# An S4 convolution block with a bilinear GLU on one Trainium2 core: another hand-written order of the first stage's side jobs, with other ring buffers

## The chip, the core and the metric

The kernel runs on one core of one Trainium2 chip. The metric is the device time of the whole program in microseconds (us), from runs on the chip; a profiled execution of the same program is the source of every view shown. The engines are named as in the profile: PE (matmuls; PEld its weight loads), DVE (vector), ACT (activations), POOL (GpSimd), SP (which issues most DMAs).

## What is computed

One input of 2048 positions (S) with D = 640 channels goes through two residual branches, each with a layer norm and a modulation from a condition c; N = 192 states, F = 1536.

```python
mod = silu(c) @ w_mod                      # six rows sa, ca, ga, sb, cb, gb of 640
h = layernorm(x) * (1 + ca) + sa
dt = exp(log_dt); P = exp(dt * A * l)      # l = 0..2047, A complex (640 x 192)
K = real(einsum("dn,dnl,dn->dl", C, P, dt * B))
y = irfft(rfft(pad(h)) * rfft(pad(K)))[:2048] + h * Dskip
x = x + ga * y
h = layernorm(x) * (1 + cb) + sb
out = x + gb * (((h @ w_gate) * (h @ w_up)) @ w_down)
```

## The kernel before

The 640 channels are NB = 5 blocks of 128 (written db below). Stage 1 makes the convolution kernel K, the transforms and the first residual (x2d, kept in DRAM); it ends at about 551 us. Stage 2 is the gated unit in two halves of 1024 positions: the `pa` matmuls of L1057 and L1459. Its order is not touched.

**The main loop of stage 1** (`for t in range(3*NK+24)`) builds K in NK = 40 kernel groups of 16 channels, eight groups to a block, three steps `t` to a group `n`:

- POOL makes the tables of group n+1 (L708): `Ph` (phases, 1536 integers a partition, buffers Pha and Phb), `EQ` (1536) and `EP` (768), both with two buffers. `EQ` of group n+2 overwrites the one of group n, so it waits until QtB(n) has read it.
- ACT turns phases into sines and cosines (`tra`, `trb`, in PSUM; L229 is the helper that issues every activation). Steps 0, 1 and 2 of a group give those for `QtA`, `PtA` and for `PtB`/`QtB`.
- DVE multiplies: `QtA(n)` (L763 to L765), `PtA(n)` (L770), `PtB(n)` (L790), `QtB(n)` (L763 to L765 again).
- PE contracts them into `kg` (L805, L820); ACT copies the result to `Kta` or `Ktb`.

**Side jobs** run between the steps: a step t has two half-steps, 2t behind ACT's part and 2t+1 behind DVE's multiplies. A generator is made for each job, and the table `SCHED` gives the numbers at which it advances by one piece. Before the change such a number v belongs to half-step v // 10 and is also the order within it; negative ones belong to the prologue's steps, and half-steps from 243 on lie behind the last kernel group, where the number only sets the order. Nothing else plans: each engine executes its instructions in the order in which this program writes them, and an instruction whose input or buffer is missing holds up all that follow on its engine.

The jobs, by the keys of `SCHED`: `ml`, `mr` load w_mod and make the modulation rows (L354, PE L361, a copy on ACT to TVa or TVb); `st` loads a slice of x and takes its statistics (L463, DVE L471 and L472, two instructions and one); `hm` normalises and stores (L483); `rstd` turns statistics into factors (L277 to L284); `fo` is the fold: ten tiny transposing matmuls into a psf buffer (L380), a chain of 11 DVE operations on 128x5 (`mcol`, L384 to L394), matmuls of L401; `e0` the second half's exponentials (`LATE`, ACT: LP seven times, RH, RL); `q`, `mc`, `low` the seeds of a block (u_seeds, u_modc) and their tables (tab_ph, tab_eq); `pre` and `g` the forward transform of h; `k` (u_k, L842) that of K, whose result ACT copies to f16b; `c` (u_c: matmul L887, DVE L928 to L934, matmul L944, ACT copies to Wa or Wb, store to WD) product and inverse transform; `d` (u_d: loads TVa or TVb from WD L957 and x L959, matmul L965, addition L969 or L972, store to x2d L973) the last transform and the residual; `h`, `w` the gated unit's head (loads `xb` from x2d L1097, statistics L1105) and the first weights (L1000, `wga`). The last block's `c` is cut in two halves of 256 columns on DVE.

**Ring buffers** are chosen by hand too: `SLOT` has for each ring a string with one letter for each tile, in the order in which the tiles are made (psf, three PSUM buffers; TV, W, f16, gh, hf, Kt, Ph, PtA, ...). A job that moves takes another place in its strings.

Of the kernel before, what the change touches and what calls it, by code (L numbers as in the profile page):

```python
# [31 lines left out]
    ml=(-885, -911, -989),  # L32
    mr=(((-871, 89), (-871, 110)), ((-874, 26), (-884, 85)), ((-886, -866), (-888, -871))),
    st=(
        (-881, 51),
        (-1006, -914),
        (51, 229),
        (-884, 159),
        (-983, 0),
        (104, 215),  # L40
        (-936, -871),
        (-978, -871),
        (17, 200),
        (3, 193),
        (-911, -870),
        (-883, 63),
        (-871, 131),
        (-990, -906),
        (-883, 169),
        (-984, -870),  # L50
    ),
    hm=(
        (-1010, 359),
        (261, 368),
        (157, 359),
        (45, 328),
        (-988, 315),
        (32, 242),
        (303, 330),
        (-877, 240),  # L60
        (214, 259),
        (147, 306),
        (259, 375),
        (324, 407),
        (425, 536),
        (528, 544),
        (445, 539),
        (356, 434),
    ),
    rstd=(229, 229),  # L70
    tab=(526, 788),
    fo=(111, 124, 196, 224),
    e0=(150,),
    ds=(325, 213, 340, 438),
    mc=((-864, 219, 303, 339, 378), (-871, 395, 451, 466, 484), (349, 569, 607)),
    q=(
# [4 lines left out]
    ),  # L81
    pre=(
# [5 lines left out]
    ),  # L88
    c=(
# [5 lines left out]
    ),  # L95
    d=(
# [5 lines left out]
    ),  # L102
    k=(
        (167, 177),
        (309, 391),
        (675, 710),
        (452, 511),
        (433, 460),
        (480, 518),
        (603, 619),  # L110
        (619, 664),
        (674, 699),
        (829, 839),
        (902, 909),
        (1092, 1097),
        (956, 974),
        (969, 1054),
        (1067, 1070),
        (1080, 1080),
        (1260, 1292),  # L120
        (1259, 1267),
        (1453, 1476),
        (1414, 1426),
        (1473, 1485),
        (1417, 1434),
        (1505, 1574),
        (1489, 1495),
        (1606, 1624),
        (1687, 1714),
        (1877, 1897),  # L130
        (1882, 1908),
        (2012, 2039),
        (2018, 2077),
        (1960, 1963),
        (1984, 2016),
        (2097, 2137),
        (2350, 2377),
        (2212, 2252),
        (2289, 2315),
        (2481, 2546),  # L140
        (2430, 2519),
        (2474, 2543),
        (2515, 2552),
    ),
    low=((146, 404, 641, 884, 1117, 1399, 1630, 1871, 2090), (182, 429, 680, 921, 1134, 1399, 1634, 1859, 2096)),
    w=(2533, 2448, 2696, 2700, 2760, 2764),
    wm=(2850, 2860),
# [11 lines left out]
    Kt="abaaabaaababababbaabababa",  # L159
# [64 lines left out]
def tile_kernel(ctx: ExitStack, tc: tile.TileContext, I, out):  # L224
# [1418 lines left out]
```

## Time and profile before

| what | value |
|---|---|
| runs of the kernel | 1009.19, 1009.78, 1012.82 us, median 1009.78 |
| profiled execution: span; end of its last instruction | 1012.8 us; 1009.8 |
| busy of the span: PE, DVE, ACT, POOL | 897.8 (89%), 765.8 (76%), 574.4 (57%), 572.4 (57%) us |
| DMA | 153.16 MB, mean 151 GB/s |
| QtA(0) starts, QtB(39) ends on DVE | 30.73, 458.55 us |
| last store to WD, first addition of the last block's d | 502.88, 512.96 us |

How to read it: times in a timeline row are start and duration in us, then engine, line, operation, output <- input, shapes and count; the bracket behind says how long the engine sat idle before the instruction and what released it. The name of a tile leaves out its number, so EQ<-LQ,RH stands for both EQ buffers. The share of busy time is a mean over both stages. PE's busy time counts pipelined matmuls whose ends are modelled.

### The profile page before, as it was taken

Reading aid. Unit: us, or ns where it says so; the run is one execution under the profiler, and the core shown is the slowest. Engines: PE = TensorE matmul, PEld = TensorE weight load, DVE = VectorE, ACT = ScalarE, POOL = GpSimd, SP = SyncE. Lnnn points to the kernel's source line nnn. Section 1 sums busy time; section 2 is a strip of 40 time slices with the busy share of each in tenths; the row PEclk is TensorE's granted clock in tenths of the full one; section 3 lists DMA queues with packets and bytes.
Section 4 is the critical chain, followed back from the end, with each engine's and each line's share of the span. In section 5 each row is a group of like instructions: output and inputs, shape, how many; then the busy total and the mean of one; then the engine's idle time right before and its main releaser. Section 6 shows DMA issues by size and latency. Waiting matters only on the chain. (4 is left out here: it accounts for less than half of the span.)

```text
span 1012.8 us, 26818 instructions
## 1 busy us (share of the span) xinstructions
PE 897.8 (89%) x11192; PEld 732.0 (72%) x11192; DVE 765.8 (76%) x1389; ACT 574.4 (57%) x1049; POOL 572.4 (57%) x423
## 2 busy tenths in 40 slices
PE   4864798799789689988888999999999999999998
PEld 3653566576576467666746788889998888889998
DVE  8698578987989987893977977787576787768452
ACT  4759999987888897872437322234464422224331
POOL 4976899799869989950035576661112354452000
PEclk9876799999979989999999999999999999999999
DMA  7654665454445553558673444524644422221341
GB/s 243 236 140 151 235 230 151 161 163 130 142 129 159 168 150 104 179 170 283 209 208 94 151 134 136 191 109 130 211 157 160 152 79 82 86 67 54 103 157 52
DMA packets 147817, 153.16 MB, mean 151 GB/s; under 512 B 9200, under 2 KB 125424, under 8 KB 146288
## 3 DMA queue, kind: packets, MB, share of 16 engines
q1 hardware_dynamic: 145968, 148.43, 46.4%
q10 hardware_dynamic: 1728, 3.02, 0.8%
q8 instruction: 88, 1.44, 0.6%
q14 instruction: 33, 0.27, 0.1%
HBM read 110.45 MB, written 40.96 MB: 150 GB/s over the span
## 5 line engine op out<-in xcount | busy, mean ns | idle before, releaser
L708 POOL TENSOR_TENSOR EQ<-LQ,RH 128x1536 f32<-128x1536 f32 x40 | 124.2, 3106 | 23.0 <-DVE QtB L765 22.8
L229 ACT ACTIVATE z<-pa 128x512 f32<-128x512 f32 x24 | 14.4, 599 | 168.6 <-PE pa L1057 120.5
L1022 DVE TENSOR_TENSOR wsgl<-wga,wsgh 128x640 fp32r<-128x640 f32 x72 | 67.9, 947 | 45.7 <-ACT wsgh L229 45.6
L229 ACT ACTIVATE wsgh<-wga 128x640 fp32r<-128x640 f32 x72 | 52.6, 732 | 66.7 <-PE pa L1459 42.7
L1408 POOL TENSOR_TENSOR z<-z,s 128x512 f32<-128x512 f32 x24 | 33.6, 1400 | 92.9 <-DVE s L1407 92.9
L1034 POOL TENSOR_TENSOR tf<-wur,wgb 128x256 f32<-128x256 f32 x24 | 18.9, 785 | 93.1 <-DVE wtl L1022 57.7
L1459 PE MATMUL pa<-wsgh,sh 128*128 128x384 f32 (+1 forms) x304 | 69.7, 310 | 0.0
L1459 PE MATMUL pa<-wsgl,sh 128*128 128x384 f32 (+1 forms) x304 | 69.2, 309 | 0.0
L1459 PE MATMUL pa<-wsgh,sl 128*128 128x384 f32 (+1 forms) x304 | 69.1, 309 | 0.0
L708 POOL TENSOR_TENSOR EP<-LP,RH 128x768 f32<-128x768 f32 x40 | 66.1, 1652 | 0.0
L708 POOL TENSOR_TENSOR Pha<-LH,DH 128x1536 int32<-128x1536 int32 (+1 forms) x21 | 62.5, 2974 | 3.7 <-ACT trb L229 3.3
L708 POOL TENSOR_TENSOR Phb<-LH,DH 128x1536 int32<-128x1536 int32 x20 | 62.3, 3115 | 3.1 <-ACT tra L229 3.1
L1022 DVE TENSOR_TENSOR wtl<-tf,wth 128x256 fp32r<-128x256 f32 (+1 forms) x72 | 60.1, 861 | 0.0
L820 PE MATMUL kg<-QtB,PtB 64*32 64x64 f32 x2560 | 48.2, 227 | 4.9 <-DVE QtB L764 4.9
L820 PEld LDWEIGHTS kg<-QtB,PtB 64*32 64x32 f32 x2560 | 41.0, 113 | 12.8 <-DVE QtB L764 6.2
L1406 DVE TENSOR_TENSOR s<-pa,s 128x512 f32<-128x512 f32 x24 | 16.6, 690 | 44.6 <-PE pa L1057 39.6
L1057 PE MATMUL pa<-sh,wtl 128*128 128x512 f32 x144 | 45.1, 395 | 4.2 <-DVE wtl L1022 4.2
L1459 PEld LDWEIGHTS pa<-wsgh,sh 128*128 128x128 f32 x304 | 46.6, 188 | 0.0
L1459 PEld LDWEIGHTS pa<-wsgh,sl 128*128 128x128 f32 x304 | 46.6, 188 | 0.0
L1459 PEld LDWEIGHTS pa<-wsgl,sh 128*128 128x128 f32 x304 | 46.6, 188 | 0.0
L1057 PE MATMUL pa<-sh,wth 128*128 128x512 f32 x144 | 44.7, 391 | 0.0
L1057 PE MATMUL pa<-sl,wth 128*128 128x512 f32 x144 | 44.5, 390 | 0.0
(576 smaller groups left out, 2953.2 us busy)
## 6 DMA issues: line engine op xcount, KB each, us to landing
wga<-wdg SPq DMA_DIRECT2D x24, 640.0 KB, 5.2
wga<-B_w_gate SPq DMA_DIRECT2D x12, 640.0 KB, 4.8
wgb<-B_w_gate SPq DMA_DIRECT2D x24, 320.0 KB, 3.3
wur<-B_w_up SPq DMA_DIRECT2D x24, 320.0 KB, 4.0
xb<-x2d SPq DMA_DIRECT2D x6, 1280.0 KB, 7.2
TVb<-WD SPq DMA_DIRECT2D x26, 256.0 KB, 3.9
t_tw<-w_mod SPq DMA_DIRECT2D x3, 1600.0 KB, 8.0
t_ti<-w_mod SPq DMA_DIRECT2D x3, 1600.0 KB, 7.6
```

The source lines that it names most:

```text
L229: return S.activation(o, i, f, **kw)
L708: G.tensor_tensor(o.rearrange("p x (h l) -> p x h l", l=8), lo.unsqueeze(2).to_broadcast([P, rows, nh, 8]), hi.rearrange("p h x -> p x h") ...
L820: PE.matmul(kg[j * 32 : j * 32 + 32, dd, :], PtB[lo : lo + 64, c, r, :], QtB[lo : lo + 64, c, r, :], start=False, stop=dd == 7 and c == 1, ...
L1022: V.tensor_tensor(lo, v, hi, op=OP.subtract)
L1034: G.tensor_tensor(t[:, 0:2], u[:, 0:2], g[:, 0:2], op=OP.subtract)
L1057: PE.matmul(ps, w[a][:, k], x[b][:, l], start=n == 0 and m == 0, stop=n == 2 and m == len(ks) - 1)
L1406: V.tensor_tensor(S67[i], ps, S6[i], op=OP.add)
L1408: G.tensor_tensor(ZT[i], ZT[i], S67[i], op=OP.add)
L1459: PE.matmul(ACC[tb][t][c], x[:, ts], w[:, cs], start=st, stop=f == NF - 1 and n == 2 and (c == 0 or t % 2 == 1))
```

## The change

Only `SCHED` and `SLOT` are rewritten, and the half-step of a number is v // 1000 instead of v // 10, so that there are a thousand places within one. The five places in `SCHED` and the line that reads it which serve as an example:

```diff
-    ml=(-885, -911, -989),
+    ml=(4000, 5, -93000),
-    rstd=(229, 229),
+    rstd=(16000, 16002),
-    fo=(111, 124, 196, 224),
-    e0=(150,),
+    fo=(16007, 18007, 19004, 23000),
+    e0=(1,),
...
-            jobs.setdefault(v // 10, []).append((v, it))
+            jobs.setdefault(v // 1000, []).append((v, it))
```

All jobs move by some half-steps; the larger ones: two of the three w_mod loads and most modulation rows leave the prologue for half-steps 0 to 15, the x statistics are dealt out anew, `e0` goes from half-step 15 to 0, the four pieces of the fold from 11, 12, 19, 22 to 16, 18, 19, 23, the table loads t_tw and t_ti from 52 and 78 to 34 and 73, the last pieces of block 3's seeds (`q`) from 124 to 134 into 125 to 132, those of block 4 from 149 to 184 into 171 to 182, and of the last block's eight halves of `c` one more is done ahead of QtB(39). The counts of instructions stay (PE 2857 rows before and after, POOL 417, SP 331, ACT 962 and 961, DVE 1236 and 1238, where the two more are groups of like instructions that are no longer neighbours). The lines of the changed file are 28 higher (L763 is L791 there).

What stands on the engines now, at three places. First DVE in the prologue, behind the first multiplications of the seeds of block 0 (L554 to L557); gha is a slice of x, DL and DH are the words of the phase tables. Before:

```order
L557 TENSOR_TENSOR pta<-pta,psfb 128x192
L593 TENSOR_TENSOR ptb<-ptb,psfa 128x192
L573 CAST psfa<-psfc 128x192
L574 CAST DL_162<-psfc 128x4x24
L577 TENSOR_TENSOR DL_162<-psfa,shl 128x12x24
```

and now:

```order
L585 TENSOR_TENSOR pta<-pta,psfc 128x192
L499 BN_STATS st_235<-gha 128x6 x2
L500 BN_AGGR mv_95<-st_235 128x2
L621 TENSOR_TENSOR ptb<-ptb,psfb 128x192
L601 CAST psfb<-psfa 128x192
L602 CAST DL_162<-psfa 128x4x24
L605 TENSOR_TENSOR DL_162<-psfb,shl 128x12x24
```

The first slice's statistics, which stood behind the seeds of the first half, stand ahead of L593 (now L621) and of the phase words.

Second ACT in the steps of group 0 (ab, tra, trb belong to the sines; TVa, TVb are modulation rows). Before:

```order
L229 ACTIVATE trb<-Pha 128x512
L229 ACTIVATE trb<-ab,halfpi 128x512
L229 ACTIVATE ab<-Pha 128x512
L229 ACTIVATE tra<-Pha 128x512
L229 ACTIVATE tra<-ab,halfpi 128x512
L229 ACTIVATE TVb<-psfc 1x384
```

and now:

```order
L257 ACTIVATE trb<-Phb 128x512
L257 ACTIVATE trb<-ab,halfpi 128x512
L257 ACT_TABLE_LOAD
L257 ACTIVATE LP_148<-RL_158 128x96 x7
L257 ACTIVATE RH_155<-RH_155 128x1056
L257 ACTIVATE RL_158<-RL_158 128x288
L257 ACTIVATE TVb<-psfa 1x384
L257 ACTIVATE ab<-Phb 128x512
L257 ACT_TABLE_LOAD
L257 ACTIVATE tra<-Phb 128x512
L257 ACTIVATE tra<-ab,halfpi 128x512
```

The exponentials of the second half stand between the sines of QtA(0) and those of PtA(0), with a table load on either side; they stood two groups later.

Third PE behind the last kernel group (L965 and L993 are the d matmuls of the second to last block, L842 and L870 those of u_k, L887 and L915 those of c's halves on f16b). Before:

```order
L965 MATMUL psfa<-TVb,ct 32x512 x4
L842 MATMUL psfb<-ct,Ktb 64x128 x8
L842 MATMUL psfc<-ct,Kta 64x128 x8
L887 MATMUL psfa<-f16b,t_tw 64x64 x16
L842 MATMUL psfb<-ct,Ktb 64x128 x8
L965 MATMUL psfc<-TVa,ct 32x512 x4
L887 MATMUL psfb<-f16b,t_tw 64x64 x16
L887 MATMUL psfa<-f16b,t_tw 64x64 x16
```

and now:

```order
L915 MATMUL psfb<-f16b,t_tw 64x64 x16
L870 MATMUL psfc<-ct,Ktb 64x128 x8
L870 MATMUL psfa<-ct,Ktb 64x128 x8
L915 MATMUL psfc<-f16b,t_tw 64x64 x16
L993 MATMUL psfb<-TVa,ct 32x512 x4
L915 MATMUL psfa<-f16b,t_tw 64x64 x16
```

The d matmul that stood ahead of three u_k groups stands behind all of them, and behind four of the halves' matmuls in place of one; its input comes through TVa, as for the d matmul before it.

More of the change, by code (lines that the diff above doesn't have):

```diff
@@ L76 @@
-    q=(
[4 rows of a table removed]
+    ml=(4000, 5, -93000),
+    mr=(((8002, 10001), (8005, 15000)), ((5000, 8006), (6, 4001)), ((-87998, 3), (-87999, 9001))),
+    st=(
+        (8003, 10000),
+        (-100000, -91000),
+        (-87000, -86999),
+        (-87996, 7),
+        (-88000, -87997),
+        (10002, 13000),
+        (8, 2000),
+        (-97999, -95000),
+        (9, 6000),
+        (8004, 12000),
+        (-86998, 4),
+        (-87995, 2),
+        (-101000, -98000),
+        (9000, 15001),
+        (8000, 8001),
+        (-86997, 0),
+    ),
@@ new lines @@
+    hm=(
+        (16011, 16011),
+        (18009, 18009),
+        (18004, 18004),
+        (19000, 19000),
+        (16003, 16003),
+        (18005, 18005),
+        (11001, 16005),
+        (11000, 16004),
+        (28000, 35000),
+        (32000, 33000),
+        (16010, 18008),
+        (16012, 25002),
+        (47001, 51001),
+        (16013, 19003),
+        (26000, 32001),
+        (40003, 51002),
+    ),
+    rstd=(16000, 16002),
+    tab=(34000, 73000),
+    fo=(16007, 18007, 19004, 23000),
@@ L81 @@
+    e0=(1,),
+    ds=(40002, 35002, 25000, 48001),
+    mc=((10003, 18003, 18006, 19002, 19005), (16001, 25003, 27000, 38000, 44001), (51000, 55000, 60001)),
+    q=(
[4 rows of a table added]
     ),
     pre=(
[5 rows of a table removed]
-    ),
-    c=(
[5 rows of a table removed]
-    ),
-    d=(
[5 rows of a table removed]
-    ),
-    k=(
[L104 to L143, printed above, removed]
-    ),
@@ new lines @@
+    d=(
[5 rows of a table added]
+    ),
+    k=(
+        (18000, 18002),
+        (16008, 16009),
+        (49000, 50001),
+        (47000, 47002),
+        (48000, 48002),
+        (49001, 50000),
+        (54002, 54003),
+        (53000, 53001),
+        (64001, 66000),
+        (86000, 86001),
+        (79001, 79003),
+        (106002, 106004),
+        (94001, 94002),
+        (92000, 92001),
+        (100000, 102000),
+        (106005, 106006),
+        (127000, 127001),
+        (112002, 112003),
+        (139002, 140000),
+        (149000, 149002),
+        (139001, 139003),
+        (140003, 145001),
+        (149001, 149003),
+        (157001, 157003),
+        (166000, 170000),
+        (160000, 160001),
+        (182008, 184000),
+        (174000, 176000),
+        (205001, 206002),
+        (201002, 206001),
+        (196000, 196001),
+        (197000, 197001),
+        (208002, 208003),
+        (229001, 231001),
+        (221001, 223000),
+        (227003, 228000),
+        (287007, 287008),
+        (241000, 287001),
+        (287014, 287016),
+        (287015, 287018),
+    ),
@@ L155 @@
+    low=(
+        (16006, 43000, 64000, 91000, 115000, 139004, 163005, 184001, 206000),
+        (21001, 40001, 67003, 89000, 117002, 137003, 165001, 188000, 210001),
+    ),
+    w=(287005, 287067, 287038, 287042, 287044, 287048),
+    wm=(287041, 287057),
+    h=(287045, 287045, 287055, 287058, 287061, 287062, 287064, 287065),
+    g=(
[5 rows of a table added]
     ),
```

90 lines of the change are left out of this document (40 added, 50 removed), and 43 rows, old and new, of tables (c, d, g, pre).

## The prediction

> **What bounds the kernel now.** I read the page's sums first, then stage 1 stretch by stretch, then the waits at its two ends. The page: busy time per engine, POOL's line in 40 slices (25 us each), the chain that ended last.
>
> ```profile
> PE 897.8 (89%) x11192; PEld 732.0 (72%) x11192; DVE 765.8 (76%) x1389; ACT 574.4 (57%) x1049; POOL 572.4 (57%) x423
> ...
> POOL 4976899799869989950035576661112354452000
> ...
> PE pa L1057 25%; PE pa L1459 16%; DMA wga<-wdg 1%; PE psg L1132 0%; DMA wdg<-xb 0%; POOL xb L1503 0%; DVE wsgl L1022 0%; DVE wtl L1022 0%; DVE sl L1022 0%; POOL a L1426 0%; ACT wth L229 0%; DVE hl L1022 0%; ACT sh L229 0%; POOL tf L1036 0%; DVE xb L1474 0%
> ```
>
> The chain's 25% and 16% are stage 2, whose matmuls the change leaves in their order. So the question is when stage 2 starts (at about 551 us, where the last stretch below ends). The next table has the span's stretches in stage 1 (PE, PEld, DVE, ACT, POOL busy, granted clock, DMA share, GB/s).
>
> ```profile
> 290.00:365.00 75.00, 60.89 (x1548) 45.02 (x1546) 68.02 (x116) 63.36 (x116) 73.06 (x41) 0.93 0.52 154
> 372.00:442.00 70.00, 64.01 (x1554) 50.35 (x1553) 57.69 (x88) 55.81 (x96) 69.45 (x36) 0.95 0.50 152
> 458.00:551.00 93.00, 76.70 (x874) 54.31 (x867) 59.97 (x153) 40.58 (x74) 15.63 (x20) 0.98 0.63 193
> ```
>
> POOL is at 9 in the slices from 125 to 175 us, and it is the fullest engine of the next two stretches (73.06 of 75, 69.45 of 70): it builds the tables of one kernel group after another and only stops for its buffers. Behind 458 POOL is out of it, and DVE idles 33 of 93 us: there the order of the side jobs sets the end. So I sum three stretches: the start until POOL binds, POOL's part to the last group, and the tail from there to stage 2.
>
> **Start.** First DVE, SP and POOL in the prologue (start, duration, what), then the landing times of the gha loads.
>
> ```profile
> 8.96 0.35 DVE L557 TENSOR_TENSOR pta<-pta,psfb 128x192 f32<-128x192 f32 x1
> 9.76 0.35 DVE L593 TENSOR_TENSOR ptb<-ptb,psfa 128x192 f32<-128x192 f32 x1 [0.45 <-ACT psfa L229]
> 17.17 0.87 DVE L471 BATCH_NORM_STATS2 st<-f16a 128x6 f32<-128x320 f32 x2
> 18.08 0.21 DVE L472 BATCH_NORM_AGGREGATE mv<-st 128x2 f32<-128x12 f32 x1
> 30.73 1.18 DVE L763 TENSOR_TENSOR QtA<-trb,EQ 128x1024 f32<-128x1024 f32 x1
> ...
> 8.10 0.52 SPq L463 DMA_DIRECT2D f16a<-A_u  x1
> ...
> DMA to landing us min/median/max: 3.3/3.7/4.1
> ...
> 26.19 3.10 POOL L708 TENSOR_TENSOR EQ<-LQ,RH 128x1536 f32<-128x1536 f32 x1
> ```
>
> The first statistics of x now stand directly behind L557, ahead of L593. DVE is there at 9.3; the load is issued at 8.10 as before and lands 3.3 to 4.1 later, at about 11.8. That is 2.0 of wait (9.76 was the next start, after 0.45 of another wait) and 1.1 of work (17.17 to 18.29): **+3** for everything behind, L593, the DL and DH words and POOL's first tables. The same work is missing later in the prologue, but a second group now stands there, so nothing comes back before EQ of group 0: 29.2 instead of 26.19.
>
> The late exponentials now run in the first step on ACT. What they cost in the old place, and the fold in the old place on DVE with POOL beside it:
>
> ```profile
> 48.20 1.28 ACT L229 ACT_TABLE_LOAD   x1
> 49.49 1.45 ACT L229 ACTIVATE LP<-RL 128x96 f32<-128x96 f32 x7
> 50.73 1.09 ACT L229 ACTIVATE RH<-RH 128x1056 f32<-128x1056 f32 x1
> 51.73 0.42 ACT L229 ACTIVATE RL<-RL 128x288 f32<-128x288 f32 x1
> ...
> 50.16 0.17 DVE L384 TENSOR_SCALAR mcol<-psfb 128x5 f32<-128x5 f32 x1 [3.68 <-PE psfb L380]
> 52.83 3.01 DVE L388 TENSOR_TENSOR mcol<-mcol 128x5 f32<-128x5 f32 x1
> 57.64 1.21 DVE L763 TENSOR_TENSOR QtA<-trb,EQ 128x1024 f32<-128x1024 f32 x1
> ...
> 52.73 3.09 POOL L708 TENSOR_TENSOR EQ<-LQ,RH 128x1536 f32<-128x1536 f32 x1
> 67.86 3.10 POOL L708 TENSOR_TENSOR EQ<-LQ,RH 128x1536 f32<-128x1536 f32 x1 [4.00 <-DVE QtB L765]
> 82.70 3.10 POOL L708 TENSOR_TENSOR EQ<-LQ,RH 128x1536 f32<-128x1536 f32 x1 [7.06 <-DVE QtB L765]
> ```
>
> The block and a table load on either side take 1.28 + 1.24 + 1.0 + 0.42 + 1.28 = 5.2 us of ACT (start to start), now between the sines of QtA(0) and those of PtA(0), where DVE has little else. With 2 of the 3 above (QtA(0) itself waits for sines, not for EQ) PtA(0) is some 7 late and QtA(1), which waited 1.25 more, some 4: 45. How the rest of the catching up goes needs the price of a group's multiplies and of the normalising factors:
>
> ```profile
> 40.72 1.22 DVE L763 TENSOR_TENSOR QtA<-tra,EQ 128x1024 f32<-128x1024 f32 x1 [1.25 <-PE kg L805]
> 46.06 0.41 DVE L765 SCALAR_TENSOR_TENSOR QtB<-tra,EQ 128x256 f32<-128x256 f32 x1
> ...
> L279 DVE RECIPROCAL rs<-ry 128x6 f32<-128x6 f32 x1 | 0.2, 192 | 0.8 <-ACT ry L229 0.8
> ```
>
> A group's multiplies take 40.72 to 46.47, 5.7. After QtA(1) at 45 come 5.7 and three statistics groups of 1.1, so QtA(2) starts at about 54 instead of 57.64: the fold's wait for psfb (3.68) and its chain (50.16 to 57.64, 7.5) have left its front. Then 5.7, two statistics groups (2.2) and the factors (14 operations of about 0.2 and 1.1 of waits, 3): QtB(2) ends at 65, so EQ(4) starts there and not at 67.86. The fold now stands behind QtB(2): 7.5, to 72.5; then QtA(3) and its group (5.7) with the four first operations of the seeds (1.5) to 80, and 1.4 that I add for waits on PE, where the last mod row now stands between. EQ(5), released by QtB(3), starts at about 81.4 and not 82.70: **−1.3**. The bounds: +8.2 if nothing of 3 + 5.2 is made up, −6.8 if the fold costs 2 (11 operations of 0.17) and not 7.5. I take −1.3: the slow row (3.01) is the one that recurs, as follows.
>
> Why the fold's operations are slow is in the rows: L388 on 128x5 takes 3.01, from 52.83 to 55.84, and POOL's EQ runs from 52.73 to 55.82. In the new place it stands directly behind QtB(2), which is what releases EQ(4): the same coincidence, so I keep 7.5. The Trainium skill, "SBUF — State Buffer", section "SBUF: two separate sides", says that VectorE operations with two SBUF inputs and GpSimd operations lock one shared port pair for a whole instruction. The row agrees with it; by the rule alone, were POOL idle there, the sum would be some 5 us lower.
>
> **POOL's part.** What is late when POOL gets full, in the slices at 125, stays late while it is. Half-steps 40 to 120 hold nearly the same work per group before and after, so −1.3 is carried. The seeds of blocks 3 and 4 move by a few half-steps: block 3's tail now stands as one lump ahead of QtA(22), and the rows behind it are relieved by the same work. No row prices that; the nearest are POOL's 7.06 of idle at a lump of the same kind (before 82.70) from above and the same 7.06 given back from below. I halve it, ±3.5, and take 0, since the work is the same. At the end one half of the inverse transform of the last block and one addition are moved ahead of QtB(39). Their prices, and where the group loop ends:
>
> ```profile
> 458.13 0.42 DVE L765 SCALAR_TENSOR_TENSOR QtB<-tra,EQ 128x256 f32<-128x256 f32 x1
> ...
> 479.84 0.69 DVE L969 TENSOR_TENSOR xb<-psfa,xsb 128x512 f32<-128x512 f32 x1 [8.28 <-PE psfa L965]
> 480.45 0.41 DVE L928 TENSOR_TENSOR TVb<-psfc,f16a 128x256 f32<-128x256 f32 x1
> 482.57 0.41 DVE L934 TENSOR_TENSOR f16a<-TVb,psfc 128x256 f32<-128x256 f32 x1
> 499.14 0.41 DVE L934 TENSOR_TENSOR f16a<-TVb,psfc 128x256 f32<-128x256 f32 x1
> ```
>
> A half is 480.45 to 482.98, 2.5; an addition 0.6: **+3.1**. The last QtB ends near 458.55 − 1.3 + 3.1 = 460.4; I go on with 461.
>
> **Tail.** DVE's 8.28 ahead of 479.84 are its largest wait there. Who holds it up, and what follows (the landing times are those of the TVb loads):
>
> ```profile
> 477.14 2.66 PE L965 MATMUL psfa<-TVb,ct 64*32 64x512 f32 x8 [4.44 <-DMA TVb<-WD]
> ...
> 481.49 0.60 ACT L229 ACTIVATE f16b<-psfb 128x512 f32<-128x512 f32 x1 [7.83 <-PE psfb L842]
> 502.88 0.33 ACTq L949 DMA_DIRECT2D WD<-Wa  x1
> ...
> 466.17 0.91 SPq L1097 DMA_DIRECT2D xb<-x2d  x2
> 467.18 2.53 SPq L957 DMA_DIRECT2D TVb<-WD  x2
> ...
> DMA to landing us min/median/max: 9.7/9.8/9.8
> ...
> 507.71 0.91 SPq L957 DMA_DIRECT2D TVb<-WD  x2
> ...
> 512.96 0.69 DVE L969 TENSOR_TENSOR xb<-psfc,xsa 128x512 f32<-128x512 f32 x1 [3.25 <-DMA xsa<-A_u]
> ```
>
> PE runs in written order. Its d matmul on TVb waits until 477.14 for a load issued at 467.18 behind two xb loads; the three u_k matmul groups (L842) behind it feed ACT's f16b (7.83 idle), and those the halves. So one half is done before DVE's wait and seven after it, 480.45 to 499.55. After the change the waiting matmul stands behind all u_k groups: four halves can be done before it, three after. The waits: QtB(39) 461, four halves and an addition to 472; the load, issued when the d matmul ahead of it has read TVa (about 465.5), again behind xb, lands some 9.8 later, so DVE's xb addition is at about 478; two halves to 484, then a wait for the third d (its load behind the two wga loads) to about 488, the last half to 490.5, and the last WD store 3.3 later, as 499.55 to 502.88: 494 to 496 with a little for the psf buffers. That is −7 to −9 on 502.88. The last block's first load follows 4.8 later as now, and the addition 5.25 after it: 504 to 506 against 512.96. The statistics of the other rows lie beside that wait, as now. I take **−7** (the three of the half are in it, since it starts from 461). Bounds: −13 if the loads land in 4 us, 0 or a loss if they become the chain.
>
> The Trainium skill, "DMA: Bandwidth & Descriptors", section "Issuing engines are not separate DMA queues", says that transfers of all issuing engines interleave on the same 16 engines. By it the W stores, now moved earlier on ACT's queue, get no lane of their own beside the wga loads; the sum by it would be −3 and not −7 (the second rival).
>
> **The sum.** The tail's figure starts from 461, so the start's −1.3 and the half's +3.1 are in it already. Stage 2 starts 7 earlier and its order is kept, so 1009.8 − 7 = **1003**. The profiled execution spans 1012.8 and its last instruction ends at 1009.8, the same as the median shown (1009.78), so no shift is needed.
>
> **Rivals.**
> 1. *POOL's start is carried* (slower, 0.23). For: POOL is full soon after its EQ(5) (82.70), so what is late there stays. Price: the 3 + 5.2 that nothing makes up, +8.2 at EQ(5) in place of −1.3, and the half's +3.1: the last QtB ends at 470. From there to stage 2 it is 551 − 458.5 = 92.5 today and 544 − 461 = 83 by my tail, so stage 2 starts at 553, +2; if the fold also keeps its wait of 3.7, +6: 1015. It decides from EQ(5) later than about 89. Against: 7.06 of idle before EQ(5) today.
> 2. *The loads are the chain* (no change, 0.21). Three d loads in a row now use the same buffer TVa, so each waits for the d matmul before it and lands up to 9.8 later; the last block's load stands behind an x2d store that waits for the last of them. 465.5 + 9.8 + 2 + 9.8 + 3 + 9.8 = 500, then the addition and store at 502 and the load at 504 to 507, against 507.71: −1 to −4; with a late group loop none. 1008.5. For: 467.18 to 477.14 is 9.96. Against: loads elsewhere are faster.
> 3. *Both ends gain* (0.12). Fold free of POOL (−5) and loads in 4 us (−13 in the tail): 994.
> 4. *It does no more than shuffle*: the engines absorb it; inside the second rival's price.
>
> **How the numbers follow.** Forecast 0.44 (1003, its own range 998 to 1007), rivals 0.23, 0.21, 0.12. About 0.5% (5 us) is what a measurement here can tell from none. Faster: the forecast without its slow edge plus the third, 0.54; slower 0.22; same 0.24. Range: 993 to 1016, which takes in the third's price and most of the first's.
>
> **What would show it.** Right: statistics at about 11.8 ahead of L593's row; EQ(5) at 80 to 83; last QtB at 458 to 462; a DVE wait before the xb addition of about 5 and not 8.3, with four halves ahead of it; last WD store at 493 to 497; stage 2 at 543 to 546. Wrong: EQ(5) past 89, or the last QtB past 465, or TV loads of over 8 us three times in a row. If the group loop ends much earlier than 458, my taking nothing from the seeds is the error.

## The result and the profile after

| what | before | after |
|---|---|---|
| median of 20 runs (range), us | 1010.03 (1003.75 to 1017.19) | 1017.91 (1012.12 to 1024.61) |
| ratio, 95% interval | | 1.0078 (1.0056 to 1.0099) |
| profiled execution, span, us | 1012.8 | 1015.1 |
| EQ(5) on POOL starts | 82.70 | 85.39 |
| last QtB ends on DVE | 458.55 | 472.34 |
| last store to WD; first addition of the last block's d | 502.88; 512.96 | 503.81; 512.93 |
| first matmul into pa | 533.21 | 533.45 |

The change is slower by 0.8%, where 0.7% faster was predicted. The two profiled executions hardly differ (2.3 us), because one execution is a draw: in the runs a time is the span plus 1.8 us (1016.91 for the span 1015.1), so the profile of before stands for about 1014.6, 4.6 above its median, and that of after about 1 below its own. So second traces of both were taken, and below a stage is read from several traces.

The page of after: busy sums, then POOL and PE's clock in slices.

```profile
PE 903.9 (89%) x11192; PEld 730.6 (72%) x11192; DVE 771.1 (76%) x1389; ACT 575.6 (57%) x1049; POOL 573.4 (56%) x423
...
POOL 4977799589969979980035576661112354452000
PEclk9969599799989779999999999999999999999999
```

The sums are those of before within 1%. No work was added; stage 1 has more waiting in it. The timeline of after at the start (DVE, ACT, POOL):

```profile
11.56 0.89 DVE L499 BATCH_NORM_STATS2 st<-gha 128x6 f32<-128x320 f32 x2 [2.48 <-DMA gha<-A_u]
14.26 0.39 POOL L719 TENSOR_TENSOR DH<-DH 128x96 int32<-128x96 int32 x1 [9.58 <-DVE DH L605]
28.67 3.10 POOL L736 TENSOR_TENSOR EQ<-LQ,RH 128x1536 f32<-128x1536 f32 x1
31.16 0.48 ACT L257 ACTIVATE TVb<-psfa 1x384 f32<-1x384 f32 x1 [2.78 <-PE psfa L389]
39.60 1.21 DVE L791 TENSOR_TENSOR QtA<-tra,EQ 128x1024 f32<-128x1024 f32 x1
53.44 1.54 DVE L305 TENSOR_SCALAR rv<-mv 128x6 f32<-128x6 f32 x1
60.20 2.96 DVE L310 TENSOR_SCALAR ry<-ry 128x10 f32<-128x10 f32 x1
63.41 0.31 DVE L312 SCALAR_TENSOR_TENSOR nm<-mv,rs 128x10 f32<-128x10 f32 x1
65.89 2.95 DVE L414 TENSOR_TENSOR mcol<-mcol 128x5 f32<-128x5 f32 x1
76.63 0.90 ACT L257 ACTIVATE ghb<-ghb,nm,rs 128x640 f32<-128x640 f32 x1
77.44 0.57 ACT L257 ACTIVATE trb<-Pha 128x512 f32<-128x512 int32 x1
85.39 3.10 POOL L736 TENSOR_TENSOR EQ<-LQ,RH 128x1536 f32<-128x1536 f32 x1 [2.09 <-DVE QtB L793]
```

To be seen: the statistics ahead of POOL's tables (EQ(0) 2.5 later than 26.19); ACT waiting 2.78 behind the late exponentials, which therefore cost nothing; the factors, 53.44 to 63.72, 10.3 us; and the last of a row of normalisations of h (0.9 each) directly ahead of sines of group 3.

And where the lateness is made, the seeds of block 2 between groups 13 and 14 (after, timeline):

```profile
204.54 0.36 ACT L257 ACTIVATE pta<-pta 128x192 f32<-128x192 f32 x1
204.95 0.49 PE L552 MATMUL psfc<-ct,pta 128*128 128x128 f32 x2 [0.54 <-ACT pta L257]
205.75 0.42 DVE L670 COPY RL<-psfc 128x96 f32<-128x96 f32 x2 [3.51 <-PE psfc L554]
206.15 0.37 POOL L730 COPY LQ<-RL 128x96 f32<-128x96 f32 x1 [11.13 <-DVE RL L670]
...
202.04 0.60 ACT L257 ACTIVATE f16a<-psfc 128x512 f32<-128x512 f32 x1 [1.12 <-PE psfc L870]
203.56 0.60 ACT L257 ACTIVATE ghb<-psfb 128x512 f32<-128x512 f32 x1 [0.93 <-PE psfb L915]
```

POOL stands 11.13 us for the RL copy, the copy for PE, PE for ACT's sine `pta`, which stands behind copies that wait for PE (the last two rows). The other four traces of the new order have this wait too, of 8.3 to 12.3. In the kernel before the copy waits for nothing; POOL's wait there is 5.57, for QtB(13), ahead of 193.42.

Start of QtB on DVE, mean of four traces whose group loop has the old order (before, b_rep, b_dmove, b_tail) and of five with the new one (after, a_rep, a_seed2, a_half, a_tail); traces of one order lie up to 8 us from their mean:

| group | 5 | 9 | 13 | 14 | 15 | 20 | 30 | 37 | 38 | 39 |
|---|---|---|---|---|---|---|---|---|---|---|
| old order | 97.9 | 146.4 | 188.9 | 195.9 | 208.0 | 257.7 | 367.0 | 434.4 | 444.9 | 454.6 |
| new order | 103.2 | 148.4 | 190.7 | 209.1 | 218.6 | 267.4 | 379.8 | 446.3 | 462.1 | 471.4 |
| later by | 5.2 | 2.1 | 1.8 | 13.2 | 10.6 | 9.6 | 12.8 | 11.9 | 17.2 | 16.8 |

Three steps: a start that is late by 5, in the mean made up to 2; 9 to 11 at groups 13 to 15; 5 at group 38. In between it changes by some 3 at most. The means hide that the start's part differs: at group 13 the first trace of after is 3.1 ahead of the first of before, the second 9.8 behind the second.

The tail of after (timeline of DVE, PE, SP, ACT's queue):

```profile
471.93 0.41 DVE L793 SCALAR_TENSOR_TENSOR QtB<-tra,EQ 128x256 f32<-128x256 f32 x1
476.71 0.42 DVE L956 TENSOR_TENSOR TVb<-psfa,f16a 128x256 f32<-128x256 f32 x1 [4.37 <-ACT f16a L257]
477.48 1.06 PE L993 MATMUL psfa<-TVa,ct 64*32 64x512 f32 x8
480.35 2.06 SPq L985 DMA_DIRECT2D TVa<-WD  x2
488.70 0.68 DVE L997 TENSOR_TENSOR xb<-psfb,xsb 128x512 f32<-128x512 f32 x1
503.81 0.33 ACTq L977 DMA_DIRECT2D WD<-Wb  x1
503.93 0.69 DVE L997 TENSOR_TENSOR xb<-psfa,xsb 128x512 f32<-128x512 f32 x1 [2.70 <-PE psfa L993]
506.01 6.28 DVE L1133 BATCH_NORM_STATS2 st<-xb 128x6 f32<-128x128 f32 x32
512.93 0.68 DVE L997 TENSOR_TENSOR xb<-psfc,xsa 128x512 f32<-128x512 f32 x1
```

From the last QtB's end to the first xb addition are 16.4 us (21.3 before), to the last block's addition 40.6 (54.4 before; 40.4 in a second trace). The tail is shorter, and it starts 13.8 later.

### The profile page after: what moved, and what is told of

Read it like the earlier page. It is cut to its first block, busy times and chain, and to the rows that moved or that the text cites. A ratio compares the mean times of both kernels' runs of the same rounds, so it can differ in the third digit from the quotient of the medians.

```text
span 1015.1 us, 26813 instructions
## 1 busy us (share of the span) xinstructions
PE 903.9 (89%) x11192; PEld 730.6 (72%) x11192; DVE 771.1 (76%) x1389; ACT 575.6 (57%) x1049; POOL 573.4 (56%) x423
## 5 line engine op out<-in xcount | busy, mean ns | idle before, releaser
L1436 POOL TENSOR_TENSOR z<-z,s 128x512 f32<-128x512 f32 x24 | 33.6, 1400 | 94.4 <-DVE s L1435 94.4
L1062 POOL TENSOR_TENSOR tf<-wur,wgb 128x256 f32<-128x256 f32 x24 | 18.9, 789 | 93.1 <-DVE wtl L1050 56.3
L736 POOL TENSOR_TENSOR Pha<-LH,DH 128x1536 int32<-128x1536 int32 x20 | 62.3, 3114 | 12.0 <-ACT tra L257 12.0
L736 POOL TENSOR_TENSOR Phb<-LH,DH 128x1536 int32<-128x1536 int32 (+1 forms) x21 | 62.5, 2975 | 3.4 <-ACT trb L257 2.7
```

Of the source, the lines that this page charges most:

```text
L736: G.tensor_tensor(o.rearrange("p x (h l) -> p x h l", l=8), lo.unsqueeze(2).to_broadcast([P, rows, nh, 8]), hi.rearrange("p h x -> p x h") ...
L1062: G.tensor_tensor(t[:, 0:2], u[:, 0:2], g[:, 0:2], op=OP.subtract)
L1436: G.tensor_tensor(ZT[i], ZT[i], S67[i], op=OP.add)
```

## Experiments

Names with b_ are made from the kernel before, with a_ from the changed one. The numbers in diffs are in the changed table's units. "First addition" is that of the last block's d.

**Second traces**, nothing edited.

> The kernel before again, for a second trace. Theory that the difference of the two profiled executions (2.3 us) is too small because the first trace of before was a slow draw: here QtB(39) ends some 3 to 5 us earlier than at 458.55, with EQ(5) near 82.7, and the execution takes about 1010. Rival, that the difference sits outside the traces: QtB(39) within 1 us of 458.55 and stage 2 within 1 us of 549.5.

Measured: 1008.07 in one run, last QtB 453.8, first addition 506.7, first matmul into pa 526.7. Every stage is 2 to 7 earlier than in the first trace of the same kernel.

> The changed kernel again, for a second trace. If its tail hides when its group loop ends: last QtB anywhere between 466 and 476, yet the first addition of the last block's d within 2 us of 512.93.

Measured: 1020.68, last QtB 477.4, first addition 517.8, 5.1 and 4.9 later than in the first trace. So the tail did not hide the lateness between these two; the expected bound of 2 us is missed.

**The new tail on the old loop** (b_tail):

```diff
-    d[3]=((247000, 255800, 255800), (244800, 245500, 252700), (242800, 244400, 246400), ...
+    d[3]=((287032, 287037, 287039), (287004, 287020, 287024), (242800, 287002, 287003), ...
```

> The kernel before with the new order of the tail alone (all that stands at half-step 243 or later, two pieces of the last block's halves at 241 and 242, and its buffers). Theory 1, that the new tail is worth what was predicted for it and the loss lies ahead of it: last QtB at 458 to 461, last WD store at 490 to 494, first addition of the last block's d at 500 to 505, 1002 us, ratio 0.992. Theory 2, that the WD store comes earlier but the last block's addition is held by other things (statistics on DVE, a fourth d): store 492 but addition 511 to 513, ratio 0.998 to 1.002. Theory 3, that the new tail itself costs: ratio above 1.003.

Measured: 1018.13, ratio 1.0082 (1.0051 to 1.0114). Last QtB 456.9, last WD store 506.07, first addition 515.0: 58.2 from the last QtB where the same tail takes 40.6 in the changed kernel. Theory 3. DVE's first waits in it:

```profile
463.96 0.69 DVE L868 TENSOR_TENSOR xsb<-psfc,xsb 128x512 f32<-128x512 f32 x1 [7.12 <-PE psfc L861]
467.49 0.42 DVE L824 TENSOR_TENSOR TVb<-psfb,f16a 128x256 f32<-128x256 f32 x1 [2.84 <-PE psfb L783]
473.63 0.42 DVE L824 TENSOR_TENSOR TVb<-psfa,f16a 128x256 f32<-128x256 f32 x1 [3.67 <-PE psfa L783]
480.23 0.69 DVE L868 TENSOR_TENSOR xsa<-psfa,xsa 128x512 f32<-128x512 f32 x1 [4.05 <-PE psfa L861]
```

All ten waits of DVE between the last QtB and the first addition sum to 25.9 us here, to 11.5 in the changed kernel (seven waits) and to 21.8 in the kernel before (eight). Behind a loop of the old order the new tail is the longest of all: what it waits for first is PE, which has 802 matmul records left up to the addition, and 602 in the changed kernel (more under "Tail" below).

**The prediction's main step alone** (b_dmove), one d matmul behind the u_k groups:

```diff
-    d[3][1]=(244800, 245500, 252700)
+    d[3][1]=(244800, 252000, 252700)
```

> The kernel before with one group of matmuls moved: the second to last block's second d matmul (8 matmuls on TVb) stands behind the three u_k groups and one half's matmuls instead of ahead of them. It is the prediction's main step alone. By the prediction: DVE's longest wait in the tail shrinks by 3 to 6, halves fill it, last WD store and the last block's first addition 3 to 6 earlier, ratio 0.994 to 0.997. Rival, that the seven halves behind it only shift in place and the next load is issued as much later: DVE's wait moves behind a later addition, ratio 0.999 to 1.002.

Measured: 1.0004 (0.9972 to 1.0036), first addition 508.7, from the last QtB 54.2 as before. The rival: no gain from the step.

**The old tail on the new loop** (a_tail, the reverse of b_tail):

> The changed kernel with before's tail (from half-step 243 on, and one half fewer ahead of the last QtB). Theory 1, that the changed group loop is late by 10 or more and the changed tail hides that, because its chain starts at something other than the last QtB: last QtB at 466 to 471, first addition of the last block's d 53 later at 519 to 524, ratio 1.012 to 1.018. Rival, that the loss is in the changed tail alone: the loop's lateness is hidden here too, first addition at 507 to 513, ratio 0.998 to 1.003.

Measured: 1.0123 (1.0081 to 1.0165). Last QtB 471.6, first addition 513.3, that is 41.8 with the old tail, and not 53. The ratio is in theory 1's range, but the trace is not: behind the new loop the old tail is about as short as the new one. That the loop is late is not the reason: b_q1, b_start2 and b_start below have late loops of the old order, and their tails take 52 to 56.

**The seeds of block 2**, alone on the old kernel (b_q1), and their last three pieces undone in the new one (a_seed2):

```diff
b_q1:
-    q[1]=(37500, 58200, 58900, 67000, 67100, 67700, 72300, 78600, 82400, 82500, 82600, 84500, 86100, 86300)
+    q[1]=(40000, 54000, 62000, 67004, 67005, 67006, 67007, 76002, 83000, 83002, 83003, 87002, 87003, 88000)
a_seed2:
-    ... 83003, 87002, 87003, 88000)
+    ... 83003, 84500, 86100, 86300)
```

> The kernel before with the seeds of block 2 alone (those between groups 8 and 14) at the places of the changed kernel; ACT's sine of pta then stands behind the hf copies and the sines of PtA, as in the changed kernel. Theory 1, that this order makes POOL wait for the RL copy and that POOL carries it: a wait ahead of POOL's LQ copy at group 14 of 6 to 11 in place of 0 to 4.6 in all there, last QtB 4 to 8 later than 454 to 458, ratio 1.004 to 1.008. Rival, that the wait needs the other side jobs around it (a cold PE, late copies): POOL's idle there under 6, ratio 0.998 to 1.002.

Measured: 1.0234 (1.0197 to 1.0271), last QtB 474.5, first addition 530.8. Against b_rep QtB(14) starts 14.2 later, QtB(15) 18.8, QtB(39) 20.7, the first addition and the first pa matmul 24.1. Dearer than expected, and carried to the end in full. The place is not the one expected: 5.6 arise ahead of group 13, and POOL waits 7.22 for QtB(13) and 8.67 ahead of an operation on `ptb`, not ahead of its LQ copy.

> The changed kernel with the last three pieces of block 3's seeds (the ones between groups 13 and 14) back at half-steps 84 and 86, where they stood before; all else as changed. Theory 1, that these three pieces make POOL's idle of 11.1 us ahead of its COPY of RL and that POOL carries it: that idle is 4 to 6, group 14 starts 5 to 8 earlier, last QtB at 464 to 467, ratio to before 1.001 to 1.003. Rival, that the start's delay is carried and this idle is only the slack that the clock made: the idle moves to another place, last QtB at 471 to 473, ratio 1.006 to 1.010.

Measured: 1.0077 (1.0042 to 1.0112), last QtB 468.4, between the two ranges. (The pieces are block 2's; the text above calls them block 3's.) POOL still waits 8.99 for the RL copy, and QtB(14) starts at 206.2. The rival in the time, but neither in the place: three pieces are not what makes the wait. No run puts all of block 2's seeds back in the changed kernel.

**The start.** b_start2 puts modulation rows, statistics, normalisations, factors, fold, late exponentials and block 0's seeds of the new order on the old kernel; b_start takes block 0's forward transforms too; a_start undoes the latter set in the new kernel.

```diff
b_start2, some of its lines:
-    rstd=(22900, 22900), fo=(11100, 12400, 19600, 22400), e0=(15000,)
+    rstd=(16000, 16002), fo=(16007, 18007, 19004, 23000), e0=(1,)
```

> The kernel before with the changed start, but block 0's forward transforms left where they were: modulation rows, statistics, normalisations, factors, fold, late exponentials and block 0's seeds at their new places. Theory 1, that the start adds 2 to 3 and POOL carries them: EQ(5) 84 to 86, last QtB 456 to 462, ratio 1.001 to 1.004. Rival, that the start's order alone gives the whole loss of the loop: last QtB past 466, ratio above 1.008. Rival, that later waits absorb it: last QtB 453 to 458, ratio 0.998 to 1.001.

Measured: 1.0164 (1.0121 to 1.0206), EQ(5) 94.4, last QtB 467.4. Against b_rep QtB(5) is 8.3 late and QtB(39) 13.6. EQ(5) is later than any theory had it; the time is the first rival's (the start alone is enough for such a loss), on the old order of what follows.

> The kernel before with the changed start: modulation rows, statistics, normalisations, factors, fold, late exponentials, block 0's seeds and forward transforms at their new places; the rest as before. Theory 1, that POOL's waits at the later seeds absorb what is late at the start: EQ(5) at 84 to 87, but the last QtB at 455 to 460, ratio 0.998 to 1.002. Rival, the prediction's first one (what is late at EQ(5) is carried while POOL is full): last QtB at 459 to 464, ratio 1.003 to 1.007.

Measured: 1.0258 (1.0207 to 1.0309), last QtB 475.4. EQ(5) is in its range, but 14 us are lost at groups 10 to 12, where PE waits 7.71 for a load of hm: two orders that do not fit. It tells nothing of the start.

> The changed kernel with before's start: modulation rows, statistics, normalisations, factors, fold, late exponentials, block 0's seeds and forward transforms at their half-steps of before; the rest as changed. Theory 1, that the order at groups 13 and 14 makes the loss: EQ(5) at 82 to 84 but last QtB at 468 to 472, ratio 1.004 to 1.008. Rival, that the start's delay is carried to the end: last QtB at 461 to 464, ratio 0.996 to 1.000.

Measured: 1.0355 (1.0318 to 1.0391), last QtB 501.1, with the loss at groups 9 to 12 again. Inconclusive for the same reason.

**Early and late halves.** b_late is the old order up to half-step 207 and the new one from there, a_late the new one up to 183 and the old one from there.

> The kernel before up to half-step 207 (group 34), and everything from 208 on in the changed order with its buffers. Theory 1, that the changed end is good (40 from the last QtB to the last block's first addition in place of 53) and the loss lies in groups 0 to 34: last QtB 458 to 464, first addition 499 to 505, ratio 0.990 to 0.996. Rival, that work was only moved from behind the last QtB to ahead of it: last QtB 464 to 470, first addition 506 to 512, ratio 0.998 to 1.003. Rival, from the run with the new tail alone: ratio 1.006 to 1.010.

Measured: 1.0068 (1.0039 to 1.0096), last QtB 467.5, first addition 512.0. Up to group 33 it keeps pace with b_rep, then POOL waits 12.1 ahead of 419 for a sine, a wait that no trace of either parent has. The loss equals the whole change's, but its place is its own. Its tail takes 44.5, against 53.0 in b_rep: what the end gains stands behind the last QtB, and the loop ahead of it lost 13.7, as the first rival has it.

> The changed kernel up to half-step 183 (group 30), and everything from 184 on in the order of before. Theory 1, that groups 0 to 30 make the loss: QtB(30) at 375 to 385 in place of 365 to 370, last QtB 466 to 474, first addition of the last block's d 519 to 525, ratio 1.010 to 1.016. Rival, that the late groups make it: first addition 508 to 513, ratio 0.998 to 1.004.

Measured: 1.0401 (1.0352 to 1.0450), last QtB 485.4, first addition 540.2, with three waits of POOL of 4.0 to 14.6 from group 31 on, and a tail of 54.8. Neither theory.

**Two small undoings in the changed kernel.**

```diff
a_hm:
-    hm[0..3]=((16011, 16011), (18009, 18009), (18004, 18004), (19000, 19000))
+    hm[0..3]=((16011, 24000), (18009, 26000), (18004, 25000), (19000, 27000))
a_half:
-    c[4][3]=(237002, 237003, 287019, ...
+    c[4][3]=(237002, 239500, 287019, ...
```

> The changed kernel with the normalisations of four of the sixteen slices (0 to 3) moved from half-steps 16 to 19 to 24 to 27, that is out of the lump that stands ahead of the sines of PtA(3) on ACT. Theory 1, that the lump makes EQ(5) late: EQ(5) 82 to 83.5 in place of 85.4, and as much earlier at group 12; ratio to before 1.003 to 1.008. Rival, that PE's matmuls or the port are what PtA(3) waits for: EQ(5) 85 to 86, ratio 1.006 to 1.010.

Measured: EQ(5) 82.5, as theory 1 has it, but last QtB 474.2 and 1.0123 (1.0091 to 1.0155), above both ranges: nothing of it reaches the end. And a_tail and a_seed2, whose start is the changed kernel's, have EQ(5) at 81.5, so one trace does not show that the lump made it late.

> The changed kernel with one half of the last block's c (six operations on DVE) put back behind the last QtB. By the prediction's term of 3.1 for it: last QtB 2.5 to 3 earlier than 472 to 477, ratio to before 1.005 to 1.008 if the tail pays it back. Rival, that the half stands in a wait anyway: last QtB within 1 of 472 to 477, tail 2.5 longer, ratio 1.008 to 1.012.

Measured: last QtB 474.0, first addition 519.8, 1.0099 (1.0061 to 1.0137). The rival: taking the half out gives nothing back.

**Work taken away, order kept.** In both kernels POOL leaves out ten of the 40 EP tables, or PE half of the kg matmuls of 28 groups:

```diff
lean:
-        mk_ep(n)
+        if n < 10 or n % 3 != 1:
+            mk_ep(n)
...
leanpe, at both places where kg is summed:
-            for c in range(2):
+            for c in range(1 if 10 <= n < 38 else 2):
```

> The kernel before without POOL's EP table in ten of the 40 groups (10, 13, ... 37), which multiply by the table of two groups earlier: 16.4 us less on POOL, nothing else changed. If POOL sets the end of before's group loop and the tail follows it: last QtB 12 to 16 earlier (440 to 445), first addition of the last block's d as much earlier, ratio 0.984 to 0.988. If DVE or the side jobs bind right behind POOL: last QtB 3 to 8 earlier, ratio 0.992 to 0.997.

Measured: 0.9987 (0.9958 to 1.0016), last QtB 458.5. Neither range: 16.4 us less on POOL gave nothing. Its stretch of groups 22 to 28, which the prediction read as POOL-bound with 73.06 of 75 busy:

```profile
290.00:365.00 75.00, 59.33 (x1466) 43.23 (x1464) 67.13 (x114) 62.40 (x115) 67.52 (x36) 0.91 0.51 152
```

POOL is down to 67.52, DVE has done as much in the same time. POOL's waits from 20 us on sum to 59.9 (44.5 before): nearly all that was taken away became idle.

> The changed kernel without POOL's EP table in the same ten groups. Theory 1, that the changed loop is late because POOL starts late and waits longer, and that its tail follows: last QtB 12 to 16 earlier than 472 to 477, ratio to before 0.992 to 0.996, the same gain as in the kernel before. Theory 2, that the changed order's side jobs and its tail form a chain of their own, which POOL no longer sets: last QtB 0 to 8 earlier, first addition 0 to 5 earlier, ratio to before 1.003 to 1.008.

Measured: 1.0062 (1.0031 to 1.0093), no difference from 1.0078 that the intervals show. Its profiled execution lies 12 above its median and is not read.

> The kernel before with half of the kg matmuls (one of the two parts, c = 0 alone) left out in groups 10 to 37: some 1.1 us less of PE in each of 28 groups at full clock, so 31 us; nothing moved. Theory now: the group loop is not set by POOL but by the ring of ACT, DVE and PE, each in its written order, and in the kernel before the chain runs mostly through ACT (about 150 of 355 us) and less through PE (90 to 115). Then last QtB is 5 to 12 earlier, ratio 0.988 to 0.996. If PE is not on it at all: 0.998 to 1.002.

Measured: 1.0030 (1.0004 to 1.0057), last QtB 460.2. Missed: PE has 1792 matmuls fewer, and there is no gain. The stretch 220 to 290 us (columns as in the prediction's table), in b_rep and here:

```profile
220.00:290.00 70.00, 59.70 (x1360) 45.06 (x1352) 61.15 (x109) 59.23 (x110) 57.36 (x39) 0.95 0.45 137
```

```profile
220.00:290.00 70.00, 59.62 (x896) 45.24 (x894) 58.07 (x103) 55.61 (x104) 54.55 (x33) 0.84 0.42 123
```

896 matmul records in place of 1360, PE busy 59.6 as before, and a granted clock of 0.84 in place of 0.95 (0.90 in the first trace of before): the clock fell with the work. Over the span it is 0.943 to 0.952 in the 12 runs, and 0.951 to 0.960 in 23 runs of the kernel before. PE's busy sum fell only to 888.2 us from 897.8 and 893.4, not by the 31 that were expected, so the run hardly took time from PE.

> The changed kernel with the same kg matmuls left out. Theory now: in the changed order the chain runs mostly through PE (140 to 185 of 370 us), at a lower clock where PE waits more; so taking PE work away gains more here than in the kernel before: last QtB 10 to 20 earlier than 472 to 477, ratio to before 0.992 to 1.001, so that the two lean kernels stand within 0.5 per cent of each other. Rival, that the loss is made by the order alone, whichever engine is lighter: the same gain as in the kernel before, 0.7 to 0.9 per cent left between the two.

Measured: 1.0068 (1.0038 to 1.0098), last QtB 477.9, granted clock 0.937 over the span (0.954 and 0.948 in the two traces of the changed kernel). Missed too: the two kernels stand 0.4% apart, but because the kernel before lost 0.3, not because the changed one gained.

## Why the prediction was wrong, step by step

**Start.** The +3 for the statistics was right (POOL's first table 14.26 against 11.49, EQ(0) +2.5). The late exponentials were priced at 5.2 on the path and cost nothing: ACT behind them waits for PE until 31.16, and QtA(1) starts at 39.60, earlier than 40.72. The factors, priced at 3 (14 operations of 0.2 and 1.1 of waits are 3.9), took 10.3, with POOL running beside them (2.96 for L310 on 128x10, at 60.20, while POOL's Phb runs from 60.02 to 63.14); the fold, priced at 7.5, took 6. The normalisations behind the factors were not priced at all. EQ(5) was forecast at 81.4 and came at 85.39; in the five traces of the new order it lies at 81.5 to 87.5, in the four of the old one at 75.4 to 82.7. The rows had the price of a tiny operation beside POOL (3.01 for L388), and I used it for the fold and not for the factors.

**POOL's part** is the step that failed: the last QtB was forecast at 461 and ended at 472.3 and 477.4, while the tail behind it came some 3 shorter than forecast. The sentences are "Half-steps 40 to 120 hold nearly the same work per group before and after, so −1.3 is carried", and, for the seeds, "I halve it, ±3.5, and take 0, since the work is the same". Block 2's seeds, inside those half-steps, were passed over since their work is the same. Their order is not: from QtB(13) to QtB(15) each of the five traces of the new loop takes 6 to 11 us more than the mean of the old one. b_q1 shows that this order by itself is enough for such a loss (20 us with the old side jobs around it); that it alone makes the loss in the changed kernel is not shown. The stretch's rows show a second thing, PE's clock (columns as in the prediction's table). Before, after and b_q1:

```profile
175.00:220.00 45.00, 39.10 (x883) 29.23 (x878) 38.65 (x63) 41.71 (x79) 38.80 (x26) 0.96 0.53 170
185.00:186.00 1.00, 1.00 (x12) 1.00 (x11) 0.97 (x2) 1.00 (x3) 1.00 (x1) 0.50 0.41 158
187.00:188.00 1.00, 0.55 (x8) 0.25 (x6) 0.97 (x3) 1.00 (x5) 0.85 (x1) 0.75 0.00 0
188.00:200.00 12.00, 11.93 (x282) 7.27 (x280) 11.18 (x21) 11.71 (x20) 6.42 (x7) 1.00 0.23 64
```

```profile
175.00:220.00 45.00, 37.48 (x780) 27.38 (x776) 31.84 (x53) 34.85 (x67) 30.89 (x23) 0.85 0.29 81
178.00:188.00 10.00, 4.92 (x125) 4.23 (x124) 9.07 (x15) 9.39 (x22) 9.88 (x4) 0.99 0.27 80
188.00:200.00 12.00, 12.00 (x156) 4.98 (x159) 8.08 (x15) 8.21 (x17) 4.70 (x2) 0.50 0.17 46
201.00:202.00 1.00, 1.00 (x18) 1.00 (x16) 0.98 (x1) 0.00 (x0) 0.00 (x0) 0.75 0.96 228
...
187.81 1.05 PE L894 MATMUL psfa<-hfb,ct 64*64 64x512 f32 x1 [3.20 <-issue]
```

```profile
175.00:220.00 45.00, 33.47 (x574) 22.43 (x567) 28.51 (x47) 32.50 (x62) 28.64 (x22) 0.73 0.39 122
```

In the changed kernel PE is half idle from 178 to 188 (4.92 of 10), the last gap being 3.20 us long, and then works without a pause at clock 0.50 until about 201.5. In the kernel before PE is as idle there (5.67 of 10, with a gap of 3.58 us ahead of 183.48), but its clock is back at 1.00 by 188, after some 3 us at 0.50. Busy time times what is missing of the clock, over 175 to 220, is 39.10·0.04 = 1.6 before (3.1 in b_rep), 37.48·0.15 = 5.6 after (5.6 in a_rep too) and 33.47·0.27 = 9.0 in b_q1. So the clock can make 2.5 to 4 of the step's 9 to 11 us; the rest is plain waiting. That it makes them is argued from these rows: no run kept PE busy there. The idle time alone does not set the clock's loss, since the kernel before has it too; why its clock comes back so much sooner stays open.

The Trainium skill, "TensorE: Matmul & The Clock Gate", Part 1, says that PE's clock halves after an idle window of about 3.4 us and comes back after about 3.4 us of sustained work. The traces agree with the halving (after gaps of 3.20 and 3.58 us). For the return the kernel before agrees, with some 3 us at 0.50, and the changed one does not: 12.00 of 12 busy passed at 0.50.

**"What is late when POOL gets full stays late."** Lateness is carried (18.8 at group 15 and 20.7 at group 39 in b_q1; 10.6 and, at group 37, 11.9 in the table), but not by POOL: b_lean. A share of 73 in 75 was that of an engine that waits in small pieces for a ring of ACT, DVE and PE, each in its written order. Which of the three sets the period stays open. Followed back from the last QtB to 100 us, as the page's chain is from the last instruction, the path lies on PE for 95 to 121 us and on ACT for 93 to 121 in the four traces of the old order (some 355 in all), and on PE for 175 to 207 and on ACT for 57 to 89 in the five of the new one (some 373). So the new order put more PE on the path. With fewer matmuls nothing was gained, but there the clock fell and PE's time with it hardly changed, so PE is not ruled out. ACT and DVE were not made lighter.

**The half ahead of the last QtB** was priced at +3.1; 5.3 arise at group 38. a_half, which puts it back, did not gain.

**Tail.** From the last QtB to the first addition 44 was forecast (461 to 505), and 40.6 and 40.4 came. The size is nearly right; the mechanism is not shown, so part of this is luck. b_dmove: the named step, alone, gives nothing. a_tail: behind the new loop the old tail, with the d matmul in its old place, takes 41.8. Over all traces the length goes with the order of the late groups (from about group 34 on), not with that of the tail, and not with how late the loop ends:

| late groups; tail | traces | last QtB | last QtB to first addition | QtB(33) to first addition | PE's matmul records behind the last QtB |
|---|---|---|---|---|---|
| old; old | before, b_rep, b_dmove, b_lean, b_leanpe, b_q1, b_start, b_start2 | 453.8 to 475.4 | 51.9 to 56.3 | 110.8 to 113.7 | 718 to 764 |
| old; new | b_tail | 456.9 | 58.2 | 121.1 | 802 |
| new; old | a_tail | 471.6 | 41.8 | 107.5 | 614 |
| new; new | after, a_rep, a_hm, a_seed2, a_half, a_start, a_leanpe | 468.4 to 501.1 | 40.4 to 45.9 | 102.0 to 108.9 | 594 to 614 |

The two spliced kernels fit: b_late, new from group 34 on, has 44.5, and a_late, old there behind a new start, 54.8. With the late groups in the new order PE owes some 100 matmuls fewer when the last QtB ends; that this is what shortens the tail is argued from the counts. The price is ahead of it: group 38 takes 14.9 in place of 10.2. From QtB(33) to the first addition the two traces of the changed kernel take 103.2 and 103.3, those of the kernel before 113.4 and 111.9. So the end of stage 1 does gain, some 9 us in these traces and less in others of the table, and the loss lies ahead: QtB(33) starts 10.2 later in the first traces and 19.6 in the second. Which of the late groups' jobs makes the difference was not separated.

In the mean of the two traces of each kernel the last QtB is 18.7 later, the first addition 5.5, stage 2's first matmul 6.4 (526.7 and 533.2 before, 533.5 and 539.2 after) and the span's end 7.4. So nearly all of the 7.9 is there when stage 2 starts. Two traces of a kernel differ by as much, so these sums are rough.

**The shift.** "No shift is needed" was right by luck: 1009.8 was the end of the last instruction, not the execution's time. The traced execution took about 1014.6, 4.6 above the median, so 7 off its time and 4.6 for the shift give 1003 all the same. (The third rival's −5 and −13 make 992, not 994; nothing hangs on it.)

**Rivals.** The first named the right side and nearly the right last QtB (470; 472.3), but its mechanism, the start's lateness carried, is not shown and at most a part: EQ(5) stayed below its 89, and a_hm brought it to 82.5 and gained nothing. On the old order a late start is carried (b_start2), and the second pair of traces has 9.8 at group 13. The second is not it either: the TVa loads take 4.7 in the median, and the load at 480.35 follows the x2d store of the addition ahead of it on SP. That the changed parts do not add up was none of my rivals: start 1.6%, block 2's seeds 2.3%, tail 0.8% and late part 0.7% alone, 0.8% together.

## What to carry to other kernels

A full engine is not a bound until work taken from it moves the end; ten left-out tables tell it in one run. In a hand-set order "the same work in the same stretch" is no reason to price a move at nothing: look for the instruction that now stands behind a wait of another engine (here a 0.36 us sine), and price the wait. And judge a tail together with the part of the loop ahead of it: here its length went with the order of the last groups (40 to 46 us, or 52 to 58), not with when the loop ended.

## What the runs showed of the hardware

- PE's clock fell to 0.50 after gaps of 3.20 and 3.58 us. It was back after some 3 us in the kernel before (184.5 to 187.5) and after some 13.5 us of unbroken work in the changed one (188 to 201.5).
- With a third of a stretch's matmuls left out (896 records for 1360) PE stayed as busy (59.6 and 59.7 of 70) at a lower clock (0.84 for 0.95).
- DVE operations on 128x5 to 128x10 took 0.17 at best and up to 2.95 and 2.96 while a POOL table ran (65.89, 60.20).
- One program on one core varies by 1.3% between executions (1003.75 to 1017.19 in 20 runs); two traces of it differ by up to 6.5 us in when a stage starts (533.2 and 526.7).
